# Sketched attention with a gated linear unit: larger transfers, another order of tokens, and a pipeline by units

## The chip, the cores and the metric

The kernel runs on one core of a Trainium2 chip. The metric is the device time of one execution in microseconds (us). Engines are named as in the profile: PE is TensorE (matmuls; PEld are its weight loads), DVE is VectorE, ACT is ScalarE, POOL is GpSimd, and SP issues most of the DMAs.

## What is computed

Two stages follow one another. The first is linear attention with a product sketch. For each of 4 batches and 4 heads, with 1088 tokens and a head dimension of 32:

```python
a = einsum('rd,bhsd->bhsr', S1, x); b = einsum('rd,bhsd->bhsr', S2, x)   # r = 8
phi(x) = outer(a, b) per token, 64 features
kv  = sum over tokens of phi(k) v          # 64 x 32 per head
z   = sum over tokens of phi(k)
out = (phi(q) kv) / (phi(q) z + 1e-6)
```

The heads' outputs side by side form x (4 x 1088 x 128) for the second stage:

```python
gate = sigmoid(causal depthwise convolution of x, 5 taps, conv_w)
result = (gate * (x @ w_val)) @ w_out
```

Inputs and result are float32.

## The kernel before, in words

**Tokens.** A batch has 1088 = 32 x 34 tokens, s = 34 j + T, with j in 0..31 (`J`) and T in 0..33 (`NT`). k and q are loaded with partitions (h, j) and columns (T, d). T is cut into three units (`U`) of 12, and a unit into four groups m of three chunks t: T = 12u + 3m + t. A 32x32 block transpose on VectorE (`block_transpose`, L172) turns a unit into `kT` or `qT`, with (h, d) on the partitions and, for each chunk t, 128 columns (m, j). So a chunk is 128 tokens.

**k_unit(b, u)** (L178): the block transpose; three matmuls `abk` (each in two passes, as float32) that give a and b for three chunks in a PSUM tile `ab`; a ScalarE copy of b into `b_sb`; one VectorE product `phik`, the outer products of 12 (chunk, head) pairs, 768 columns; and six `kv` matmuls (12 passes) that add phik^T v for two pairs of heads into the PSUM tile `kv`. v carries a block of ones, so that z comes out of the same matmuls.

**k_finish(b)** (L209), after a batch's three units: `rz` and the `zs` matmuls fold z with S2 into the third part of `rhsq` (by a ScalarE copy), so that a matmul with `rhsq` gives a, b and a factor c with sum of a*c = the denominator. Then `kvb` (kv masked, bf16), `wg` (kv times the convolution's taps: attention output and convolution become one matmul), and `kw` = kv w_val by a transpose and two matmuls.

**q_phi(b, u)** (L253): block transpose, three `abq` matmuls, the copy `a_sb`, then on VectorE `prod` = a*c, its row sum `den`, the reciprocal `rden`, `an` = a/den and the outer products `phiq` (bf16). Six TensorE transposes put phiq into the PSUM tile `pt`, and one ScalarE copy into `phiT`, columns ordered by T, with a halo of four T in front. For u = 2 two GpSimd copies fill that halo from the batch's last four T, moved by one j.

**q_out(b, u)** (L303), for T = 12u to 12u + 11: ten `g_ps` matmuls (five taps, two head pairs) over shifted columns of phiT, two `v_ps` matmuls with kw, the sigmoid `gate`, the VectorE product `gv`, three `o_ps` matmuls with w_out, the copy `o_sb`, and four DMAs to the output, one for each m.

**Order.** The text runs the three k units of batch 0 and k_finish(0), then for each batch q_phi 2, q_phi 0, k unit 0 of the next batch, q_out 0, q_phi 1, and so on (L347 to L363). Each engine executes its own list of instructions in order, with semaphores between engines. That list is not the order of the text: the framework plans it, by its own costs for each instruction, by the readiness of inputs and free buffers, and gives what stands earlier in the text precedence. Tiles of the pool `work` have three buffers (`o_sb` among them). In PSUM there are 2 buffers for `ab`, 1 for `kv`, 2 for `pt`, 3 for the rest (`ps_g`).

**Loads** go through SP's queue in the text's order: for each batch three for k, 24 for v (`load_v`, L84, 24 KB each) and three for q; the stores follow on the same queue. ScalarE's queue has the eight small S_blk loads (S1 and S2 transposed by the access pattern, into a block-diagonal matrix), s_l2 and wm; GpSimd's has the two weights, cast to bf16. GpSimd clears and fills the constants first (L75 to L163).

## Time and profile before

| | |
|---|---|
| median of 3 runs | 118.78 us (118.59 to 119.14) |
| the profiled execution | 118.95 us |
| its span, first to last instruction | 117.2 us |
| mean granted TensorE clock | 0.885 |
| DMA | 9.29 MB, 17544 packets, 12928 of them under 512 bytes |

A profile is one execution. A row such as "27.20 0.66 PE L257" in order of time gives the start, the time to the end of the group, the engine and the line of the kernel; "x12" counts instructions, where a float32 matmul counts twice. A row of a group gives busy time and the mean of one in nanoseconds (ns), then the idle time of the engine ahead of it and what ended most of that. The rows "PE" and "PEclk" of the profile's second part cut the span into 40 slices of 2.93 us and show tenths. "SPq" and "ACTq" are the parts of those engines that issue DMAs and wait.

### The profile page before, as it was taken

To read this page: it belongs to the slowest core of one execution; us is meant where nothing else is said; L and a number is where in the kernel's file an instruction comes from. 1 tells how busy PE (TensorE), PEld (TensorE's weight loads), DVE (VectorE), ACT (ScalarE), POOL (GpSimd) and SP (SyncE) were. 2 spreads that over 40 slices of the span, in tenths; PEclk is the share of its full clock that TensorE was granted. 3 is DMA by queue.
4 is the path that set the end of the run, shared out by engine and by line. 5 is a ranking of instruction groups with operands and counts; after the bars stand their busy time and mean duration, and the time that the engine had idled before them with its cause. 6 is when DMAs were issued, how large, how long until landed. Compare 5 with 4: busy or idle time off the path is not lost.

```text
span 117.2 us, 1742 instructions
## 1 busy us (share of the span) xinstructions
PE 78.9 (67%) x568; PEld 64.3 (55%) x568; DVE 54.4 (46%) x125; ACT 31.7 (27%) x78; POOL 12.1 (10%) x55
## 2 busy tenths in 40 slices
PE   0009029998399559985699998665799667668720
PEld 0008029986385447954687696555699326355300
DVE  0300073516944622576648555876930511884110
ACT  0000500004155321124243401434120224476330
POOL 7909700000010000000010000010000000010000
PEclk9999999999955876999557999999756999999995
DMA  2831424832238422383222730000010022222222
GB/s 75 154 46 38 86 53 118 270 90 51 49 82 279 107 51 53 89 282 97 52 51 62 244 102 11 0 0 0 0 50 17 0 71 58 67 74 52 67 67 56
DMA packets 17544, 9.29 MB, mean 79 GB/s; under 512 B 12928, under 2 KB 17536, under 8 KB 17536
## 3 DMA queue, kind: packets, MB, share of 16 engines
q1 hardware_dynamic: 13440, 8.92, 28.6%
q10 hardware_dynamic: 3808, 0.21, 2.1%
q0 software_dynamic: 288, 0.07, 0.6%
q8 instruction: 4, 0.07, 0.3%
q14 instruction: 4, 0.03, 0.1%
HBM read 7.02 MB, written 2.23 MB: 79 GB/s over the span
## 4 chain that ended last, share of the span: by engine, by line
PE 55%; DVE 15%; DMA 10%; ACT 9%; issue 4%; ACTq 1%; SPq 1%; DVEq 0%
PE kv L200 19%; PE g_ps L309 11%; PE abq L257 8%; PE abk L184 5%; DVE phiq L274 5%; PE pt L285 5%; PE v_ps L319 4%; DMA S_blk<-in_S_dram 3%; ACT phiT L290 3%; DVE phik L192 3%; DMA k_sb<-in_k_dram 2%; DMA v_sb<-in_v_dram 2%; PE zs L220 2%; ACT gate L324 2%; DVE kT L173 2%
## 5 line engine op out<-in xcount | busy, mean ns | idle before, releaser
L184 PE MATMUL abk<-S_blk,kT 128*128 128x64 f32 x72 | 13.7, 342 | 15.4 <-DMA v_sb<-in_v_dram 8.8
L200 PE MATMUL kv<-v_sb,phik 128*128 128x96 f32 x144 | 24.1, 339 | 0.0
L200 PEld LDWEIGHTS kv<-v_sb,phik 128*128 128x128 f32 x144 | 23.4, 253 | 0.7 <-issue 0.5
L184 PEld LDWEIGHTS abk<-S_blk,kT 128*128 128x128 f32 x72 | 12.9, 259 | 16.0 <-issue 14.6
L192 DVE TENSOR_TENSOR phik<-abk,b_sb 128x768 f32<-128x768 f32 x12 | 11.4, 955 | 15.7 <-ACT b_sb L188 15.7
L309 PE MATMUL g_ps<-phiT,wg 128*64 128x384 bf16 x120 | 14.8, 379 | 2.0 <-ACT phiT L290 1.5
L328 DVE TENSOR_TENSOR gv<-gate,v_ps 128x384 bf16<-128x384 bf16 x12 | 6.6, 553 | 16.3 <-PE v_ps L319 9.3
L285 PE MATMUL pt<-identity,phiq 128*128 128x128 bf16 x72 | 7.3, 250 | 9.6 <-DVE phiq L274 9.6
L290 ACT COPY phiT<-pt 128x768 bf16<-128x768 bf16 x12 | 9.6, 799 | 13.4 <-PE pt L285 13.3
L257 PE MATMUL abq<-rhsq,qT 128*128 128x96 f32 x72 | 12.0, 307 | 0.5 <-ACT rhsq L224 0.5
L285 PEld LDWEIGHTS <-phiq 128*128 128x128 bf16 x72 | 5.4, 114 | 11.3 <-DVE phiq L274 10.9
L257 PEld LDWEIGHTS abq<-rhsq,qT 128*128 128x128 f32 x72 | 10.4, 215 | 1.7 <-issue 1.1
L274 DVE TENSOR_TENSOR phiq<-an,abq 128x768 bf16<-128x768 f32 x12 | 11.2, 942 | 0.1
L298 POOL COPY phiT<-phiT 128x124 bf16<-128x124 bf16 x8 | 2.1, 290 | 88.5 <-ACT phiT L290 88.5
L324 ACT ACTIVATE gate<-g_ps 128x384 bf16<-128x384 f32 x12 | 5.9, 490 | 18.1 <-PE g_ps L309 18.1
L309 PEld LDWEIGHTS <-wg 128*64 128x64 bf16 x120 | 7.2, 122 | 5.5 <-ACT phiT L290 1.2
L319 PE MATMUL v_ps<-phiT,kw 128*128 128x384 bf16 x24 | 6.8, 370 | 1.7 <-ACT gate L324 1.7
L173 DVE STREAM_TRANSPOSE kT<-k_sb 128x384 f32<-128x384 f32 x12 | 6.7, 566 | 2.6 <-DMA k_sb<-in_k_dram 2.6
L264 DVE TENSOR_TENSOR prod<-a_sb,abq 128x96 f32<-128x96 f32 x12 | 3.0, 253 | 8.9 <-ACT a_sb L261 8.8
L173 DVE STREAM_TRANSPOSE qT<-q_sb 128x384 f32<-128x384 f32 x12 | 6.1, 555 | 2.2 <-DMA q_sb<-in_q_dram 2.2
L339 ACT COPY o_sb<-o_ps 128x384 f32<-128x384 f32 x12 | 5.7, 478 | 5.0 <-PE o_ps L334 3.9
L334 PE MATMUL o_ps<-w_out_sb,gv 128*128 128x128 bf16 x36 | 4.1, 221 | 3.3 <-DVE gv L328 3.3
(46 smaller groups left out, 49.8 us busy)
## 6 DMA issues: line engine op xcount, KB each, us to landing
v_sb<-in_v_dram SPq DMA_DIRECT2D x88, 24.0 KB, 1.8
out_dram<-o_sb SPq DMA_DIRECT2D x44, 48.0 KB, 1.6
k_sb<-in_k_dram SPq DMA_DIRECT2D x8, 192.0 KB, 3.7
q_sb<-in_q_dram SPq DMA_DIRECT2D x8, 192.0 KB, 2.5
k_sb<-in_k_dram SPq DMA_DIRECT2D x4, 160.0 KB, 3.9
q_sb<-in_q_dram SPq DMA_DIRECT2D x4, 160.0 KB, 3.3
wm<-in_moe_conv_w_dram ACTq DMA_DIRECT2D x4, 40.0 KB, 2.7
S_blk<-in_S_dram ACTq DMA_DIRECT2D x8, 1.0 KB, 2.5
```

The source lines that it names most:

```text
L173: nc.vector.transpose(out=dst[:, u * W : (u + 1) * W].rearrange("p (t m j) -> p t m j", t=NCK, m=M4), in_=src[:, u * W : (u + 1) * W].rear ...
L184: nc.tensor.matmul(ab[:, 0:2, t, :], lhsT=chunk_of(kT[b], u, t), rhs=S_blk, start=True, stop=True)
L192: nc.vector.tensor_mul(phik, a_v.unsqueeze(3).to_broadcast([P, NCK * H, r, r]), b_v.unsqueeze(2).to_broadcast([P, NCK * H, r, r]),)
L200: nc.tensor.matmul(kv_ps[b][:, g], lhsT=phik[:, x : x + 2].rearrange("p h i j -> p (h i j)"), rhs=v_sb[b][:, u, 3 * g : 3 * g + 3, t, :], ...
L257: nc.tensor.matmul(ab[:, :, t, :], lhsT=chunk_of(qT[b], u, t), rhs=rhsq[b], start=True, stop=True)
L274: nc.vector.tensor_mul(phiq, an.unsqueeze(3).to_broadcast([P, NCK * H, r, r]), ab[:, 1].rearrange("p t (h j) -> p (t h) j", h=H) .unsqueeze(2)
L285: nc.tensor.transpose(pt[:, g, :, t, :], phiq[:, x : x + 2].rearrange("p h i j -> p (h i j)"), identity,)
L290: nc.scalar.copy(out=phiT[b][:, :, HALO + u * W : HALO + (u + 1) * W], in_=pt.rearrange("p g m t j -> p g (m t j)"),)
L309: nc.tensor.matmul(g_ps[2 * D * g : 2 * D * (g + 1), :], lhsT=wg[b][:, g, kk, :], rhs=phiT[b][:, g, off : off + W], start=(kk == 0), stop= ...
L319: nc.tensor.matmul(v_ps, lhsT=kw[b][:, g, :], rhs=phiT[b][:, g, c0 : c0 + W], start=(g == 0), stop=(g == 1),)
L324: nc.scalar.activation(out=gate.rearrange("p m t j -> p (m t j)"), in_=g_ps, func=ACT.Sigmoid)
L328: nc.vector.tensor_mul(gv.rearrange("p t m j -> p m t j"), gate, v_ps.rearrange("p (m t j) -> p m t j", m=M4, t=NCK),)
```

## The change

- **Tokens.** T = 9m + 3u + t. A partition group m now holds nine T of all three units; a unit takes three from each group. So the k and q tiles keep T in order, and v's tile is laid out by (x, 9 T, d). phiT stays ordered by T, so its copy from `pt` is scattered over the groups and done in two instructions, and each q_out needs the columns of all three units of its batch.
- **Transfers.** k and q come by one DMA a batch (k of batch 0 in three units, the last with a remainder), v by eight; six output units go by one DMA each, the other six by four.
- **S.** S1 and S2 are loaded as rows (`s_nat`), transposed by TensorE, and spread over the block diagonal `S3` by two VectorE products with a head mask. S3 has a third block of zeros, so abk has 96 columns.
- **Shared outer products.** In k_unit ScalarE copies a and b (`ab_sb`); VectorE makes the products of two chunks (`phik`, 512 columns) and GpSimd those of the third (`phip`, 256 columns).
- **Denominators.** `ac` copies a and c; GpSimd makes `prod` and `an`, VectorE keeps `den` and `rden`. q_phi is split: `q_den` up to `an`, `q_phi` from `phiq` on.
- **k_finish.** ScalarE copies kv to `kvs`; GpSimd makes `kvb` and `wg` of it; `kw` is one matmul with a masked w_val of 256 columns, and one copy.
- **Order.** One loop over 19 steps with, in step s, q_den of unit s - 3, k_unit of unit s, q_phi of unit s - 4, q_out of unit s - 7, and k_finish after each third k unit.
- **Others.** The pool of `ab` has 3 buffers, `pt` 1. A sigmoid on a dummy column stands early on ScalarE. The constants' memsets on GpSimd are put in another order, and the s_l2 and wm loads come after them in the text.

```diff
-    J, NT, U, TU, M4, NCK = 32, 34, 3, 12, 4, 3
+    J, NT, U, M4, NCK = 32, 34, 3, 4, 3
+    TU = M4 * NCK
+    TM = U * NCK
...
+    def load_all(src, dst, b):
+        nc.sync.dma_start(out=dst[:, : NT * D], in_=kq_rows(src, b))
...
+    load_unit(k, k_sb[0], 0, 0)
+    for x, Sx in enumerate((S1, S2)):
+        nc.scalar.dma_start(
+            out=s_nat[x * r : (x + 1) * r], in_=Sx.unsqueeze(1).to_broadcast([r, H, D])
+        )
+    for u in range(1, U):
+        load_unit(k, k_sb[0], 0, u)
+    load_v(0)
+    load_all(q, q_sb[0], 0)
...
+    nc.scalar.activation(out=warm, in_=warm, func=ACT.Sigmoid)
+    for b in range(B):
+        nc.gpsimd.memset(k_sb[b][:, NT * D :], 0.0)
+        nc.gpsimd.memset(v_sb[b][:, 2:6:3, :, :], 1.0)
+        nc.gpsimd.memset(v_sb[b][3 * J :, :, NT - 3 * TM :, :], 0.0)
+        if b == 0:
+            nc.gpsimd.memset(s_l2, 0.0)
+            nc.gpsimd.memset(wm, 0.0)
...
+    st_ps = ps_g.tile([P, 2, r], F32, tag="g", name="st_ps")
+    nc.tensor.transpose(
+        st_ps.rearrange("p x r -> p (x r)"), s_nat.rearrange("p h d -> p (h d)"), identf
+    )
...
+        nc.vector.tensor_mul(
+            S3[:, x].rearrange("p (h r) -> p h r", h=H),
+            st_ps[:, x].unsqueeze(1).to_broadcast([P, H, r]),
+            hm.unsqueeze(2).to_broadcast([P, H, r]),
+        )
...
     for b in range(1, B):
-        for u in range(U):
-            load_qk(k[b], k_sb[b], u)
+        load_all(k, k_sb[b], b)
         load_v(b)
-        for u in range(U):
-            load_qk(q[b], q_sb[b], u)
+        load_all(q, q_sb[b], b)
...
+        ab_sb = work.tile([P, 2, NCK * HR], F32, tag="ab_sb", name="ab_sb")
+        nc.scalar.copy(out=ab_sb, in_=ab[:, 0:2].rearrange("p x t c -> p x (t c)"))
...
+        outer(nc.vector, phik, ab[:, 0, :nd].rearrange("p t (h i) -> p (t h) i", h=H), ab_sb[:, 1], 0, nd * H)
+        outer(
+            nc.gpsimd, phip, ab_sb[:, 0].rearrange("p (x i) -> p x i", i=r)[:, nd * H :], ab_sb[:, 1],
+            nd * H, H,
         )
...
-        kvb = work.tile([P, 2, 2, D], BF16, tag="kvb", name="kvb")
-        nc.vector.tensor_mul(
-            kvb, kv[:, :, 0:2, :], m64.unsqueeze(1).to_broadcast([P, 2, 2, D])
+        kvs = work.tile([P, 2, 2 * D], F32, tag="kvs", name="kvs")
+        nc.scalar.copy(out=kvs, in_=kv[:, :, 0:2, :].rearrange("p g x d -> p g (x d)"))
+        kvb = work.tile([P, 2, 2 * D], BF16, tag="kvb", name="kvb")
+        nc.gpsimd.tensor_mul(
+            kvb, kvs, m64.rearrange("p x d -> p (x d)").unsqueeze(1).to_broadcast([P, 2, 2 * D])
         )
...
+        kw_ps = ps_g.tile([P, 2, P], F32, tag="g", name="kw_ps")
+        nc.tensor.matmul(kw_ps, lhsT=kvt, rhs=w_val_sb, start=True, stop=True)
...
-        a_sb = work.tile([P, NCK * H, r], F32, tag="a_sb", name="a_sb")
-        nc.scalar.copy(out=a_sb, in_=ab[:, 0].rearrange("p t (h i) -> p (t h) i", h=H))
+        ac = work.tile([P, 2, NCK * H, r], F32, tag="ac", name="ac")
+        nc.scalar.copy(out=ac, in_=ab[:, 0:3:2].rearrange("p x t (h i) -> p x (t h) i", h=H))
...
+        nc.gpsimd.tensor_mul(prod[:, :, 0:r], ac[:, 0], ac[:, 1])
...
-        nc.vector.tensor_mul(an, a_sb, rden.unsqueeze(2).to_broadcast([P, NCK * H, r]))
+        nc.gpsimd.tensor_mul(an, ac[:, 0], rden.unsqueeze(2).to_broadcast([P, NCK * H, r]))
...
-        nc.scalar.copy(
-            out=phiT[b][:, :, HALO + u * W : HALO + (u + 1) * W],
-            in_=pt.rearrange("p g m t j -> p g (m t j)"),
-        )
+        for g in range(2):
+            nc.scalar.copy(
+                out=phiT[b][:, g, HALO:].rearrange("p (m u x) -> p m u x", m=M4, u=U)[:, :, u],
+                in_=pt[:, g].rearrange("p m t j -> p m (t j)"),
+            )
...
+        if u < U - 1 and not last:
+            nc.sync.dma_start(
+                out=o_d[:, T0 : T0 + TU, :].rearrange("j (m t) e -> m j (t e)", m=M4),
+                in_=o_sb.rearrange("p t e -> p (t e)"),
+            )
+            return
...
+    N = B * U
+    LQ, LP, LO = U, U + 1, 2 * U + 1
+    for s in range(N + LO):
+        if 0 <= s - LQ < N:
+            q_den(*divmod(s - LQ, U))
+        if s < N:
+            k_unit(*divmod(s, U))
+        if 0 <= s - LP < N:
+            q_phi(*divmod(s - LP, U))
+        if 0 <= s - LO < N:
+            q_out(*divmod(s - LO, U))
+        if s < N and s % U == U - 1:
+            k_finish(s // U)
```

## The prediction

> **What bounds the kernel now.** I read the page's totals first, then busy time by stage (cut where each batch's first abq matmul starts), then the order of time.

> ```profile
> PE 78.9 (67%) x568; PEld 64.3 (55%) x568; DVE 54.4 (46%) x125; ACT 31.7 (27%) x78; POOL 12.1 (10%) x55
> ```
> ```profile
> 18.10:27.20 9.10, 8.51 (x44) 8.10 (x43) 3.85 (x9) 0.57 (x3) 0.00 (x0) 1.00 0.56 158
> 27.20:51.10 23.90, 18.25 (x127) 14.82 (x127) 13.12 (x32) 7.63 (x19) 0.52 (x2) 0.79 0.40 105
> 51.10:72.20 21.10, 18.20 (x142) 14.82 (x143) 13.11 (x32) 6.50 (x17) 0.52 (x2) 0.84 0.39 108
> 72.20:98.20 26.00, 19.08 (x142) 15.92 (x142) 13.43 (x32) 7.14 (x19) 0.52 (x2) 0.87 0.08 21
> 98.20:110.60 12.40, 9.21 (x86) 6.10 (x87) 6.71 (x18) 6.73 (x16) 0.52 (x2) 1.00 0.24 61
> ```
> The second list has, by stretch, its length and the busy time of PE, weight loads, DVE, ACT, POOL, then the granted clock. TensorE is the engine nearest to its limit, in every batch; no other passes 62% of a batch. But 27.2 us go by before the first abq, the batches take 23.9, 21.1 and 26.0 us for like work, and the clock is below 1 in all three. Each has a cause in the order of time. The start, two steps of the chain of waits and then the rows in order of time (start, length, work):

> ```profile
> 0.81 2.51 DMA k_sb<-in_k_dram
> ...
> 3.35 3.46 DMA S_blk<-in_S_dram
> ```
> ```profile
> 1.04 5.45 ACTq L100 DMA_DIRECT2D S_blk<-in_S_dram  x8
> 6.89 3.15 ACTq L110 DMA_DIRECT2D s_l<-in_S_dram  x4
> 10.13 2.71 ACTq L116 DMA_DIRECT2D wm<-in_moe_conv_w_dram  x4
> 12.87 1.28 ACT L188 ACT_TABLE_LOAD   x1 [12.87 <-DMA v_sb<-in_v_dram]
> 14.16 0.38 ACT L188 COPY b_sb<-abk 128x96 f32<-128x96 f32 x2
> 18.19 7.74 PE L200 MATMUL kv<-v_sb,phik 128*128 128x96 f32 x36
> 27.20 0.66 PE L257 MATMUL abq<-rhsq,qT 128*128 128x96 f32 x4 [0.30 <-ACT rhsq L224]
> ```
> ScalarE issues 16 DMAs and loads a table before its first copy, at 14.16; the kv matmuls, 215 ns each, start only at 18.19. (The granted clock there reads 1.00, while the same 36 take 6.76 in a stretch at half clock, below. So I take the matmuls' own pace for the first stage.) Batch 2 has the SP queue behind it:

> ```profile
> 50.78 12.11 SPq L92 DMA_DIRECT2D v_sb<-in_v_dram  x24
> 64.43 50.86 SPq L344 DMA_DIRECT2D out_dram<-o_sb  x48
> ```
> ```profile
> out_dram<-o_sb SPq DMA_DIRECT2D x44, 48.0 KB, 1.6
> ```
> ```profile
> 64.38 0.33 PE L334 MATMUL o_ps<-w_out_sb,gv 128*128 128x128 bf16 x3
> 85.37 0.49 ACT L339 COPY o_sb<-o_ps 128x384 f32<-128x384 f32 x1
> ```
> The 120 loads, all ahead of the first store, keep SP until 64.4 (a store itself lands in 1.6). Only three o_sb exist, so the fourth copy stands at 85.37, 21 us after its o_ps, and the three ps_g banks stay filled. The planner orders the engines: abk and kv are written in turn by unit, yet the kv of batch 0 and of batch 3 run as one lump of 36.

> **Prices of TensorE.** From the chain of waits and the kv lines by stretch, first at full, then at half clock:

> ```profile
> 78.93 0.51 PE pt L285 x6
> 79.44 0.70 PE abq L257 x6
> 80.13 0.66 PE abk L184 x6
> ...
> 94.12 0.34 PE o_ps L334 x3
> ...
> 91.40 0.95 PE g_ps L309 x10
> ```
> ```profile
> 66.90:71.10 4.20, 4.12 (x34) 3.84 (x34) 1.00 0.35 90
> ```
> ```profile
> 56.70 0.82 PE pt L285 x6
> ...
> 59.44 1.33 PE abq L257 x6
> 60.77 1.74 PE g_ps L309 x10
> ...
> 66.63 0.43 PE v_ps L319 x2
> ...
> 71.31 0.63 PE zs L220 x4
> ...
> 84.64 6.76 PE kv L200 x36
> ```
> A unit at full clock: abq 0.70, abk 0.66, kv 12 x 4.12/34 = 1.45, pt 0.51, g 0.95, v 0.43, o 0.34, together 5.04. A k_finish: zs 0.63 and some 0.4 for the transpose and kw, an estimate: 1.0. At half clock the unit is 1.33 + 1.33 + 2.25 + 0.82 + 1.74 + 0.75 (v scaled like g) + 0.34 = 8.56, 1.7 times as much.

> Batch 1 (21.1 us) thus did 3 x 5.04 + 1.0 = 16.1 us of full-clock work: 76%. Its mean clock of 0.84 lost 0.16 x 21.1 = 3.4 us; without it the share is 16.1 / 17.7 = 91%. Over the whole body, 27.2 to 110.6, the work is 9 k units x 2.11 + 12 q units x 2.93 + 3 x 1.0 = 57.2 in 83.4 us: 69%.

> **The change part by part.**

> *The start.* Two s_nat DMAs replace eight; at 5.45/8 = 0.68 us each the second is issued by 2.4, and with a landing of 2.5 (the k load takes 2.51) there by 5, against 3.35 + 3.46 = 6.8. One transpose (bounded by pt's 0.1 each and a lone matmul's 0.3) and two small DVE products (near rz, under 0.3 each) make S3 by about 5.6. k's first unit now comes in 384-byte pieces, four times as many. Between 2.5 us (same bytes) and the S_blk landing (3.46, also many small pieces), I take 3.5, so kT is done by 5 and abk (1.4 at the slow pace) by 7. The table load goes ahead under the landing DMAs. But s_l2 and wm, 3.15 + 2.71 = 5.9 us of issue, still stand before the first copy in the written order, and wait for GpSimd's memsets: from about 3.6, ScalarE is free at 9.5. The copy then comes at 9.5 instead of 14.16, phik at 10.6.

> ```profile
> L157 POOL MEMSET v_sb<- 128x576 f32 x4 | 2.3, 580 | 0.0
> ...
> L163 POOL COPY rhsq<-S_blk 128x64 f32<-128x64 f32 x4 | 1.0, 238 | 2.8 <-DMA v_sb<-in_v_dram 2.8
> ...
> L160 POOL MEMSET k_sb<- 128x64 f32 x4 | 0.6, 156 | 0.2
> ...
> L298 POOL COPY phiT<-phiT 128x124 bf16<-128x124 bf16 x8 | 2.1, 290 | 88.5 <-ACT phiT L290 88.5
> ...
> L192 DVE TENSOR_TENSOR phik<-abk,b_sb 128x768 f32<-128x768 f32 x12 | 11.4, 955 | 15.7 <-ACT b_sb L188 15.7
> ...
> L264 DVE TENSOR_TENSOR prod<-a_sb,abq 128x96 f32<-128x96 f32 x12 | 3.0, 253 | 8.9 <-ACT a_sb L261 8.8
> ```
> GpSimd's setup (these memsets four times, a third weight DMA, wider masks) is longer than now, done near 13, and phip of unit 0 stands behind it. So kv: 24 from 10.6 at 215 ns to 15.8, the last 12 to 18.4, abq 1.2 later (as now, 25.94 to 27.20): **19.6**. Early end: kv at 121 ns, GpSimd not late, 10.6 + 4.4 + 1.2 = 16.2. Late end: kv in one lump behind three phips (14.5 + 7.7 + 1.2), 23.4.

> *GpSimd's products.* No two-input product stands in GpSimd's trace. Lower bound: a memset's slope, (580 - 156)/512 = 0.83 ns an element plus 0.1. Upper: a copy's (290 - 238)/60 = 0.87 twice, one read after the other, plus 0.18. A copy is the nearer row, with two inputs in place of one, so the upper: 256 elements 0.63 us, 96 0.35, 128 0.40, 320 0.74. A unit's phip, prod and an are 1.33; a batch's kvb, two wg and the halo copies 0.40 + 1.48 + 0.52; a batch 6.4 of some 17 us. It is no bound, and DVE loses phik 768 to 512 (slope (955 - 253)/672: 0.27), prod and an (0.51) a unit. What queues behind a waiting GpSimd instruction is phip, so kv's last third, and den on DVE; each has a step's work of other kinds ahead of it.

> *ScalarE.* ab_sb and ac carry 192 columns for 96, phiT goes in two copies: some 0.08 + 0.08 + 0.16 a unit, 4 us in all over 32, beside TensorE; were it on the path, 4 us.

> *The pipeline.* q_den is now a step ahead of q_phi, q_out three behind it. That takes the 2.3 us waits of pt for phiq (den, rden, an, phiq in line) off TensorE. A third ps_ab bank carries it; ps_pt falls to one, so pt waits for the two phiT copies of the unit before, a step old: nothing, or at most 0.96 x 12 us without that cover. q_out(b,0) now needs all three q_phi of its batch; the lag covers it but for the end, where three q_out stand behind the last phiT, not two: 1.7 us, inside the share taken below.

> *k_finish.* kvb now goes through a copy of kv (0.27, as kvt's 128 columns) and GpSimd, wg too: some 2 us from kv to wg instead of 1.3. Nobody asks for wg or kw before q_out, five steps on; without that lag it would be 0.7 x 4 us. The zs path to abq is unchanged. One kw matmul replaces two.

> *SP.* 43 loads for 120, at 12.11/24 = 0.50 us, are issued by 22 us; the larger ones keep the DMA engines busy longer, some ten microseconds by the same bytes (an estimate). Stores then start when o_sb is there, so the 21 us hold goes. Stores fall from 48 to 30; the last batch keeps four a unit.

> *The end.* o_sb 0.49, four issues at 0.50, a landing 1.6, and 0.5 to the last instruction (an estimate): 4.6 behind the last o_ps.

> **The sum.** Body: 9 x 2.15 (abk at abq's price, as 96 columns) + 35.2 + 3.0 = 57.5 us. The pipeline should do better than batch 1's 76% and has light first steps and a tail against 91%. I take the middle, 83%: 69.3. So 19.6 + 69.3 + 4.6 = 93.5 of span; the profiled execution took 118.95 with a span of 117.2, 1.75 around it: **95 us**, against 118.95 (median of the runs 118.78). With 91% it is 89.2, with 76% 101.6; with the bounds of the start 85.8 to 105.4.

> **Rivals.**

> *Only the start is won.* The written order is not the order that runs (kv's lumps). If the planner undoes the steps as it did the units, the body stays at 69%: 57.5 / 0.69 = 83.3, so 109 us. Against it: SP's block, which made batch 2 the longest, goes in any order.

> *GpSimd held off by DVE.* If each of the 24 transposes (0.57 us) delays a product that TensorE waits for, 13.7 us come on top, 109. [...]

> *Slower: the low clock.* The clock fell each time after TensorE had been thin, as these slices of 2.93 us show:

> ```profile
> PE   0009029998399559985699998665799667668720
> ...
> PEclk9999999999955876999557999999756999999995
> ```
> Slice 10 (counted from 0) has PE at 3 tenths, and 11 and 12 have the clock at 5; slices 18 and 19 are at 5 and 6, and 19 to 21 have 5, 5, 7; slices 25 to 27 (6, 6, 5) are followed by 7, 5, 6. If the finer pipeline leaves TensorE with many short gaps, low stretches join. With 91% and a low share f, the body is 57.5 x (1 + 0.69 f)/0.91; it makes up the whole 93.0 us that are left to it (118.95 less 19.6, 4.6 and 1.75) at f = 0.68. Three quarters low gives 122. Before had 0.23 low (a mean clock of 0.885); more constant work speaks against it. [...]

> **How the numbers follow.** Forecast 0.70, better than 84 us 0.04 (share above 91% and the early start), only the start 0.12, GpSimd held 0.06, low clock 0.06, no change 0.02. The range 84 to 109 holds the forecast, GpSimd held and half of the only-start case, 0.82. Half a per cent is about what a measurement can tell from no change; faster is 0.92, the same 0.02, slower 0.06.

> **What would show it.** First b_sb/ab_sb copy near 9.5 and abq near 19.6; a store before 60 us; no o_sb copy more than 3 us behind its o_ps; GpSimd's 256-element product at 0.3 to 0.63; batches of 17 to 20 us; clock above 0.9. Wrong if PE's share of a full batch falls below 70%, or GpSimd ends most of its idle time.

## The result, and the profile after

The changed kernel takes 91.83 us (median of 4 runs, 91.51 to 95.51), the kernel before beside it on the same chip 118.96 us (118.59 to 119.50). The ratio is 0.771, 95% interval 0.766 to 0.775. The forecast was 95 us, the range 84 to 109. The kernel before has two kinds of executions, of about 116.2 us at a granted clock of 0.905 and of 117 to 120 us at 0.857 to 0.892; all of them here are of the second kind, and against the first, as in the ratios below, the changed kernel has 0.789. The profiled execution took 91.90 us with a span of 90.2, at a mean granted clock of 0.982 instead of 0.885.

The totals of the page of the changed kernel, and TensorE with its clock in 40 slices of 2.26 us:

```profile
PE 68.8 (76%) x565; PEld 55.5 (62%) x565; DVE 42.4 (47%) x97; ACT 33.8 (37%) x90; POOL 37.4 (42%) x103
...
PE   0119699979699699999988599999698767666600
...
PEclk9999999999999999999999999999999999999975
```

The stretches of the changed kernel, cut where the first abq matmul of each batch starts, then the work behind them (length and busy time of PE, weight loads, DVE, ACT, POOL; then the clock, the DMA engines' share and GB/s):

```profile
20.30:33.20 12.90, 11.06 (x96) 10.02 (x96) 8.93 (x19) 4.70 (x15) 6.07 (x13) 1.00 0.80 220
33.20:47.80 14.60, 13.80 (x126) 11.76 (x126) 9.60 (x22) 7.24 (x21) 6.25 (x14) 1.00 0.06 16
47.80:65.00 17.20, 15.52 (x143) 12.74 (x143) 8.99 (x19) 8.45 (x25) 7.76 (x16) 1.00 0.13 33
65.00:75.40 10.40, 8.33 (x79) 5.55 (x79) 5.45 (x12) 5.90 (x16) 3.25 (x9) 1.00 0.15 38
75.40:85.60 10.20, 7.17 (x63) 3.22 (x63) 2.22 (x4) 4.30 (x10) 0.58 (x2) 1.00 0.30 83
```

TensorE's busy time fell from 78.9 to 68.8 us though it has nearly the same matmuls: what went is the half clock, which in the kernel before lay on 23.8 us between 32.2 and 90.2 (TensorE busy for 22.1 of them) and of which no stretch here shows any (it comes at 87.0, behind the last o_ps). The lag of q_out moves work to the end, so the first two batches are short; only the third, 17.2 us, holds three units of every kind. In the kernel before it took 26.0 us.

The start of the changed kernel in order of time (start, length, work):

```profile
7.42 2.68 ACTq L192 DMA_DIRECT2D wm<-in_moe_conv_w_dram  x4
...
6.33 4.16 PE L222 MATMUL abk<-S,kT 128*128 128x96 f32 x18 [2.31 <-DVE S L174]
...
10.14 0.76 ACT L226 COPY ab_sb<-abk 128x192 f32<-128x192 f32 x3 [6.86 <-POOL phiT L167]
...
20.34 0.46 PE L304 MATMUL abq<-rhsq,qT 128*128 128x96 f32 x2 [0.28 <-ACT rhsq L272]
```

ScalarE's first copy stands behind its own wm loads (7.42 + 2.68 = 10.10). "POOL phiT", named as what released it, is a memset of a tile that the copy doesn't read.

### The profile page after: what moved, and what is told of

Same layout as the page of the kernel before. It is cut to its first block, busy times and chain, and to the rows that moved or that the text cites. A ratio compares the mean times of both kernels' runs of the same rounds, so it can differ in the third digit from the quotient of the medians.

```text
span 90.2 us, 1666 instructions
## 1 busy us (share of the span) xinstructions
PE 68.8 (76%) x565; PEld 55.5 (62%) x565; DVE 42.4 (47%) x97; ACT 33.8 (37%) x90; POOL 37.4 (42%) x103
## 2 busy tenths in 40 slices
DMA packets 9137, 9.29 MB, mean 103 GB/s; under 512 B 4649, under 2 KB 8233, under 8 KB 9129
## 3 DMA queue, kind: packets, MB, share of 16 engines
q1 hardware_dynamic: 7112, 8.92, 35.2%
## 5 line engine op out<-in xcount | busy, mean ns | idle before, releaser
L248 PE MATMUL kv<-v_sb,phik 128*128 128x96 f32 x96 | 16.0, 316 | 2.6 <-DVE phik L229 1.8
L248 PEld LDWEIGHTS kv<-v_sb,phik 128*128 128x128 f32 x96 | 14.4, 226 | 3.7 <-DVE phik L229 3.5
L222 PE MATMUL abk<-S,kT 128*128 128x96 f32 x72 | 12.4, 315 | 3.1 <-DVE S L174 2.3
L341 ACT COPY phiT<-pt 128x384 bf16<-128x384 bf16 x24 | 10.7, 484 | 6.9 <-PE pt L335 6.9
L222 PEld LDWEIGHTS abk<-S,kT 128*128 128x128 f32 x72 | 11.0, 226 | 3.7 <-DVE S L174 2.4
L379 DVE TENSOR_TENSOR gv<-gate,v_ps 128x384 bf16<-128x384 bf16 x12 | 6.6, 551 | 11.6 <-ACT gate L375 10.4
L313 DVE TENSOR_REDUCE den<-prod 128x12 f32<-128x108 f32 x12 | 3.2, 264 | 16.1 <-POOL prod L311 16.1
L311 POOL TENSOR_TENSOR prod<-ac 128x96 f32<-128x96 f32 x12 | 4.7, 389 | 13.8 <-ACT ac L308 13.8
L229 DVE TENSOR_TENSOR phik<-abk,ab_sb 128x512 f32<-128x512 f32 x12 | 7.7, 656 | 4.3 <-ACT ab_sb L226 4.2
L229 POOL TENSOR_TENSOR phip<-ab_sb 128x256 f32<-128x256 f32 x12 | 7.4, 625 | 3.5 <-ACT ab_sb L226 3.4
L248 PE MATMUL kv<-v_sb,phip 128*128 128x96 f32 x48 | 8.5, 306 | 0.0
L308 ACT COPY ac<-abq 128x192 f32<-128x192 f32 x12 | 3.9, 322 | 9.9 <-PE abq L304 9.3
```

The costliest lines, as they stand in the source:

```text
L222: nc.tensor.matmul(ab[:, :, t, :], lhsT=chunk_of(kT[b], u, t), rhs=S3, start=True, stop=True)
L229: eng.tensor_mul(dst, a.unsqueeze(3).to_broadcast([P, n, r, r]), bb.rearrange("p (x j) -> p x j", j=r)[:, lo : lo + n] .unsqueeze(2) .to_b ...
L248: nc.tensor.matmul(kv_ps[b][:, g], lhsT=src.rearrange("p h i j -> p (h i j)"), rhs=v_sb[b][:, 3 * g : 3 * g + 3, NCK * u + t, :], start=(u ...
L341: nc.scalar.copy(out=phiT[b][:, g, HALO:].rearrange("p (m u x) -> p m u x", m=M4, u=U)[:, :, u], in_=pt[:, g].rearrange("p m t j -> p m (t ...
L379: nc.vector.tensor_mul(gv.rearrange("p t m j -> p m t j"), gate, v_ps.rearrange("p (m t j) -> p m t j", m=M4, t=NCK),)
```

## The experiments

The changed kernel was timed again beside three of the ten variants: 91.43 us (90.86 to 91.94), ratio 0.789 (0.780 to 0.797). The variants are compared with it by these ratios, in which 0.010 is 1.2 us, and by their medians where the executions lie close together. An edit can also change the order that the planner makes of the rest of the text, which matters in some cases below.

> The changed kernel once more, as the yardstick for the three beside it on the same chip: 91 to 92.5.

### The order of the steps, alone and taken back

In the kernel before, the loop of the changed kernel, with q_phi split and 3 and 1 buffers for `ab` and `pt`; transfers and engines as before. In the changed kernel, the loop of before as far as its dependences allow:

```diff
-        q_phi(b, 2)
-        q_phi(b, 0)
-        if b + 1 < B:
-            k_unit(b + 1, 0)
...
+    for s in range(N + LO):
+        if 0 <= s - LQ < N:
+            q_den(*divmod(s - LQ, U))
+        if s < N:
+            k_unit(*divmod(s, U))
```

> The kernel before with the new loop of 19 steps, q_den split from q_phi and 3 + 1 PSUM buffers for ab and pt; its loads, token order, start and VectorE products stay. If the order makes most of the body's gain, the body's share goes from 69% towards 80% but the o_sb hold stays: 105 to 110, with a clock above 0.93. If the transfers make it, 116 to 120.

> The changed kernel with an order like the old one (three k units and k_finish first, then by batch q_den and q_phi together, k units of the next batch and q_out between them); transfers, start and GpSimd's products stay. If the order carries the body: share of 76%, body 76 against 65, so 100 to 104. If the transfers carry it: 92 to 95.

The new order alone: 107.67 us (105.92 to 111.27), ratio 0.919 (0.902 to 0.935), so 0.081 x 116.2 = 9.4 us less. The old order in the changed kernel: 103.04 us (101.24 to 108.04), ratio 0.873 (0.868 to 0.877), 0.084 over the 0.789, so 9.8 us more. The order carries some 10 us either way. TensorE's waits in the changed kernel (in all, times, longest), first as it is:

```profile
PE pt L335 <- DVE phiq L324: 0.9, 3, 0.3
```

and with the old order, with its clock from the page:

```profile
PE pt L335 <- DVE phiq L324: 7.5, 5, 2.0
...
PE g_ps L360 <- POOL phiT L349: 2.3, 2, 1.4
```
```profile
PEclk9999975999999999999999999999999995555555
```

pt waits 7.5 us instead of 0.9 for phiq, g_ps 2.3 for GpSimd's halo copies, and the last seven slices run at half clock. So the order is worth these waits and what they do to the clock.

### Output tiles of their own

```diff
-        o_sb = work.tile([P, NCK, P], F32, tag="o_sb", name="o_sb")
+        o_sb = ctile([P, NCK, P], F32, f"o_sb{b}_{u}")
```

> The kernel before with twelve o_sb tiles in place of three, so that no copy of o_ps waits for a store; the stores still start behind the loads near 64 us. If the o_sb hold is a term of its own, batch 2 falls from 26.0 to the 21 of batch 1 and the last store wait (1.1) goes: 112 to 114. If TensorE is held elsewhere and the hold is harmless, 118 to 119.

114.88 us (113.70 to 116.59), ratio 0.980 (0.975 to 0.985): the hold of o_sb behind SP's loads is a term, of some 2 us (0.020 x 116.2 = 2.3). In the stretches of this variant, batch 2 and what follows it:

```profile
72.20:91.70 19.50, 15.44 (x143) 12.72 (x143) 13.38 (x31) 7.15 (x20) 0.52 (x2) 1.00 0.16 43
91.70:114.00 22.30, 13.00 (x98) 8.34 (x98) 7.26 (x19) 7.33 (x17) 0.52 (x2) 0.85 0.12 33
```

Batch 2 loses 6.5 of its 26.0 us, as the prediction's reading of 85.37 says. But the rest takes 22.3 us where it had 19.0 (98.2 to 117.2), 6.8 us of it at half clock (97.0 to 103.8), so half of the gain is given back.

### Small loads in the changed kernel

```diff
-                nc.sync.dma_start(
-                    out=v_sb[b][J * m : J * (m + 1), 3 * g : 3 * g + 2, :n, :],
+                for u in range(U):
...
+                    nc.sync.dma_start(
+                        out=v_sb[b][J * m : J * (m + 1), 3 * g : 3 * g + 2, NCK * u : NCK * u + n, :],
...
-        nc.sync.dma_start(out=dst[:, : NT * D], in_=kq_rows(src, b))
+        for lo in range(0, NT * D, TU * D):
+            hi = min(lo + TU * D, NT * D)
+            nc.sync.dma_start(out=dst[:, lo:hi], in_=s[:, lo:hi])
```

> The changed kernel with the loads cut up again, each transfer a third as large: v in 24 transfers a batch instead of 8, k and q of every batch in three instead of one. Order, engines and arithmetic are those of the changed kernel. Theory 1 (the large transfers carry nothing once the loads lie ahead of the stores): 91 to 93 us beside 91.4 of the changed kernel, and the waits of the body unchanged. Theory 2 (the number of issues on SP sets when the data come): the queue of SP takes about 0.6 us an issue, 80 more issues are up to 48 us of SP, so the loads of batch 2 and 3 come 20 us or more later than the 30.2 us at which SP was done, and the time is 95 us or more, with a wait for v_sb or k_sb inside the body.

101.83 us (101.08 to 104.74), ratio 0.872 (0.863 to 0.881): theory 2 by the time, some 10 us more, far above what the hold of o_sb explains. Theory 1 had been drawn from that hold alone. But the longest wait stands ahead of the body, not inside it as theory 2 has it, and not all of the 10 us is the loads themselves. The variant's rows in order of time, the stretch of its batch 0, and what pt waits for:

```profile
2.95 13.12 SPq L111 DMA_DIRECT2D v_sb<-in_v_dram  x24
...
16.11 1.38 SPq L102 DMA_DIRECT2D q_sb<-in_q_dram  x3
17.53 1.38 SPq L102 DMA_DIRECT2D k_sb<-in_k_dram  x3
...
15.18 0.71 PE L254 MATMUL kv<-v_sb,phik 128*128 128x96 f32 x2 [4.93 <-issue]
...
24.99 0.46 PE L310 MATMUL abq<-rhsq,qT 128*128 128x96 f32 x2 [0.28 <-ACT rhsq L278]
```
```profile
25.00:43.10 18.10, 14.06 (x96) 13.22 (x96) 8.49 (x19) 5.48 (x16) 6.63 (x15) 0.81 0.41 102
```
```profile
PE pt L341 <- DVE phiq L330: 7.1, 7, 2.2
```

An issue takes 13.12/24 = 0.55 us, so the 19th of the 24, which the first kv needs as it is the first of the last partition group, is issued near 13.3 and lands some 2 us later (2.0 is the median of these loads up to 26 us). TensorE waits 4.93 us and starts kv at 15.18 instead of 11.24 ("issue" means that the profile shows no releaser; that it is v is worked out from these times). Batch 0's q and batch 1's k are issued only from 16.1 on; in the changed kernel those two are issued at 6.92 and 9.05:

```profile
2.96 3.91 SPq L105 DMA_DIRECT2D v_sb<-in_v_dram  x8
6.92 0.59 SPq L99 DMA_DIRECT2D q_sb<-in_q_dram  x1
9.05 0.35 SPq L99 DMA_DIRECT2D k_sb<-in_k_dram  x1
...
29.76 0.43 SPq L99 DMA_DIRECT2D q_sb<-in_q_dram  x1
```

The first abq comes 4.65 us later, about as much as kv, and batch 0 takes 18.1 instead of 12.9 us. (This profiled execution took 104.74 us, 2.9 above the median. Two stretches of half clock of 3.4 us each lie in its batch 0, which the two executions with a mean clock of 0.99 can't have had, so some 3 of these 5 us are not in the 10.) The pieces are smaller as well as more, 12040 packets under 512 bytes instead of 4649, but from 6.0 to 25 us, the stretch with this wait, the DMA engines' share is 0.48 (0.83 in the changed kernel from 6.3 to 20.3), so it was the issuing that held.

The rest of the 10 us comes with another planned order. The text is that of the changed kernel, but the kv of batches 1 and 2 stand together here, all 36 of a batch with nothing between them, where the changed kernel has them in three parts; and pt waits 7.1 us for phiq instead of 0.9. The new order alone, with the small loads of the kernel before, has the same lumps:

```profile
57.23 4.21 PE L200 MATMUL kv<-v_sb,phik 128*128 128x96 f32 x36
```

So the planner spreads kv over the steps with the large loads of the changed kernel and not with the small ones, and the two parts of the change are not independent. How the rest of the 10 us divides between late loads and planned order is not shown.

### GpSimd's products on VectorE

```diff
-        nd = NCK - 1
+        nd = NCK
...
-        nc.gpsimd.tensor_mul(prod[:, :, 0:r], ac[:, 0], ac[:, 1])
+        nc.vector.tensor_mul(prod[:, :, 0:r], ac[:, 0], ac[:, 1])
```

and likewise an, kvb and wg.

> The changed kernel with phik in one product of 768 columns, prod, an, kvb and wg all on VectorE; GpSimd keeps memsets and halo copies. VectorE goes from 42 to about 57 us of 90. If its relief is no part of the gain: 90 to 94 (the start gains 1 to 2 us, as kv no longer waits behind GpSimd's memsets). If the sharing with GpSimd carries the body: above 99.

89.61 us (89.24 to 90.34), ratio 0.772 (0.766 to 0.779) where the changed kernel has 0.789; by the medians 1.8 us less than 91.43. VectorE is busy 61% of its span, which sets nothing. So the sharing brings no time and costs a little (two variants of the end, below, are 1.9 us apart by the same edit). The start is not the place. The first abq is at 19.38 instead of 20.34, but kv starts at 11.54, later than the 11.24 of the changed kernel, and in the second profile of the changed kernel, without any edit, the first abq is at 19.62:

```profile
16.65 1.34 PE L248 MATMUL kv<-v_sb,phik 128*128 128x96 f32 x8
...
19.62 0.46 PE L304 MATMUL abq<-rhsq,qT 128*128 128x96 f32 x2 [0.28 <-ACT rhsq L272]
```

These eight kv take 1.34 us, where the same eight, from 16.68 in the first profile, take 1.92: what differs is when the slow pace of the start ends. From the first abq to the last o_ps the changed kernel has 64.9 us in both profiles, this variant 62.7, and there the gain lies. Which product costs it is not shown, as the planned order differs too. What GpSimd's products took in the changed kernel, by groups:

```profile
L229 POOL TENSOR_TENSOR phip<-ab_sb 128x256 f32<-128x256 f32 x12 | 7.4, 625 | 3.5 <-ACT ab_sb L226 3.4
L281 POOL TENSOR_TENSOR wg<-kvs,wm 128x320 bf16<-128x320 f32 x8 | 6.7, 862 | 0.0
L311 POOL TENSOR_TENSOR prod<-ac 128x96 f32<-128x96 f32 x12 | 4.7, 389 | 13.8 <-ACT ac L308 13.8
L317 POOL TENSOR_TENSOR an<-ac,rden 128x96 f32<-128x96 f32 x12 | 4.2, 352 | 3.1 <-DVE rden L315 2.8
L276 POOL TENSOR_TENSOR kvb<-kvs,m 128x128 bf16<-128x128 f32 x4 | 1.8, 456 | 10.1 <-ACT kvs L274 10.1
```

### An earlier start

ScalarE's s_l2 and wm loads go to SP's queue, behind batch 0's q; GpSimd's memsets of batches 1 to 3 go behind the phip of the batch before.

```diff
-            nc.scalar.dma_start(
+            nc.sync.dma_start(
                 out=s_l2[
...
-            nc.scalar.dma_start(
+            nc.sync.dma_start(
                 out=wm[
...
+        if s % U == 2 and s // U + 1 < B:
+            clear(s // U + 1)
```

> The changed kernel with s_l2 and wm issued by SP behind batch 0's loads, and the memsets of batches 1 to 3 on GpSimd put behind phip of batch 0. The first ab_sb copy comes at 7.9 instead of 10.1 and phip at 8.5 instead of 12.5. If the first stage then runs at TensorE's slow pace of some 220 ns (54 instructions from 6.3), kv ends only 0.7 us earlier: 91. If ScalarE's issues and GpSimd's queue set its end: 2 to 4 us less, 88 to 90.

100.13 us (99.64 to 100.81), ratio 0.863 (0.856 to 0.871) against the 0.789 of the changed kernel beside it: both theories missed. The first abq did come 3.2 us earlier, at 17.17. Its rows in order of time, and its stretches from the fall of the clock on, 3.4 us each but for the last, which ends 0.2 before the return (as above; the clock is the third number from the end):

```profile
17.17 0.64 PE L312 MATMUL abq<-rhsq,qT 128*128 128x96 f32 x4
...
22.05 0.82 PE L343 MATMUL pt<-identity,phiq 128*128 128x128 bf16 x6 [3.88 <-DVE phiq L332]
22.67 1.54 PE L230 MATMUL abk<-S,kT 128*128 128x96 f32 x6
...
32.30 0.72 PE L343 MATMUL pt<-identity,phiq 128*128 128x128 bf16 x5 [1.62 <-DVE phiq L332]
```
```profile
19.20:22.62 3.42, 0.57 (x6) 0.57 (x7) 1.97 (x5) 0.00 (x0) 1.81 (x3) 0.50 0.98 336
22.62:26.03 3.41, 3.41 (x19) 3.41 (x17) 1.47 (x3) 1.50 (x4) 0.73 (x2) 0.50 0.83 163
26.03:29.45 3.42, 3.42 (x17) 3.26 (x17) 2.31 (x5) 0.64 (x2) 1.61 (x4) 0.50 0.69 244
29.45:32.86 3.41, 1.79 (x15) 1.55 (x13) 2.40 (x5) 1.18 (x3) 0.97 (x2) 0.50 0.97 259
32.86:36.27 3.41, 3.41 (x18) 3.41 (x17) 0.79 (x2) 0.00 (x0) 0.00 (x0) 0.50 0.44 151
36.27:39.45 3.18, 3.18 (x17) 3.18 (x16) 0.00 (x0) 0.00 (x0) 0.00 (x0) 0.50 0.00 0
```

TensorE waited 3.88 us for the first phiq, and from 19.2 to 39.6 the clock was at half: six abk matmuls took 1.54 us, where the changed kernel has 0.83 to 0.91. It fell 1 us into the wait, not at its end, and the low stretch of 20.5 us is six times 3.41, the step on which the clock of the kernel before changes as well (last section). TensorE was busy throughout the second, third and fifth of the stretches above (3.41, 3.42 and 3.41 us), and the clock came back only behind the sixth. What brings it down or back is not shown.

First I held GpSimd for the cause: its `an`, which phiq needs, stood behind two wg products of 0.86 us. The same start with every product on VectorE tests that.

> The variant of the earlier start (ScalarE's two loads on SP, the clears of the later batches behind), 100.13 us, with every product of GpSimd moved to VectorE. Theory 1 (what cost the 8.7 us there was TensorE's 3.88 us wait for the first phiq behind GpSimd's two wg products, after which the granted clock stayed near 0.6 for some 16 us): on VectorE the products don't queue behind wg on GpSimd, no wait near 22 us is over 1.5 us, the clock stays over 0.95 and the time is 86 to 89 us, below the 89.6 of the kernel with all products on VectorE and the old start. Theory 2 (the loads of s_l2 and wm that now stand behind batch 0's on SP come too late, whoever multiplies): a wait for wm of about the same length stays, and the time is 97 to 101 us.

91.51 us (90.61 to 93.00), ratio 0.778 (0.775 to 0.782): 8.6 us less by the medians, but neither theory, as it is 1 to 2 us above the same products with the late start (89.61), and the wait is still there. In order of time:

```profile
18.60 0.43 SPq L99 DMA_DIRECT2D k_sb<-in_k_dram  x1
...
20.34 0.95 DVE L327 TENSOR_TENSOR phiq<-an,abq 128x768 bf16<-128x768 f32 x1
21.21 1.49 DVE L219 STREAM_TRANSPOSE kT<-k_sb 128x384 f32<-128x384 f32 x3
21.35 0.82 PE L338 MATMUL pt<-identity,phiq 128*128 128x128 bf16 x6 [3.37 <-DVE phiq L327]
```

GpSimd's queue was 0.5 of the 3.88 us. For the rest, TensorE had nothing else to do. In the changed kernel kT of batch 1 is transposed from 13.83 on and its abk fills the time of den, rden, an and phiq:

```profile
13.83 1.50 DVE L211 STREAM_TRANSPOSE kT<-k_sb 128x384 f32<-128x384 f32 x3
```

Here the eight small loads of s_l2 and wm hold SP from 7.24 to 12.74, so batch 1's k is issued at 12.79 (9.05 in the changed kernel), and the planner put its transposes behind phiq and its abk behind pt. With GpSimd out, the clock was at half for only 6.8 us, 19.4 to 26.3 (twice 3.4). That is 13.7 us less of half clock, at half the pace up to 6.8 us, so most of the 8.6 (an estimate). Why the low stretch is three times as long with GpSimd's products, the runs don't show; the planned orders of the two variants differ too. A second wait for phiq (1.62 us near 31) lies inside it, but the two stretches ahead of that, 3.41 and 3.42 us with TensorE busy throughout, had not brought the clock back either.

### A warm TensorE

```diff
+    wz = ctile([P, 512], BF16, "wz")
+    nc.vector.memset(wz, 0.0)
...
+    busy(9)     # nine 512-column matmuls of zeros ahead of the transpose of S
```

> The changed kernel with nine matmuls of zeros (bf16, 512 columns, into a spare PSUM tile) on TensorE ahead of the transpose of S. If the slow pace of the first stage is a clock that activity raises, abk and kv of batch 0 take 120 ns instead of 220 and kv ends behind phip near 15 instead of 19.2: 87 to 89. If the pace is set by the loads that land in that stage, 91.5 to 92.5.

91.90 us (91.33 to 95.22): no gain, and yet it was work ahead of them that the slow first matmuls lacked. The variant in order of time:

```profile
1.79 3.57 PE L175 MATMUL wps<-wz 128*128 128x512 bf16 x9 [1.79 <-DVE wz L170]
...
6.16 2.25 PE L232 MATMUL abk<-S,kT 128*128 128x96 f32 x18 [0.64 <-DVE S L184]
11.18 1.67 PE L258 MATMUL kv<-v_sb,phik 128*128 128x96 f32 x8 [2.77 <-DVE phik L239]
```

The 18 abk take 2.25 us instead of 4.16, 125 ns each instead of 231. Then TensorE waits 2.77 us, as ScalarE's first copy is still at 10, and the kv run at 1.67/8 = 209 ns again. From 11.6 to 18.4 this variant's record has the clock at 0.50, and eight kv take 1.92 us there, as long as those of the changed kernel at 14.12, whose record reads 1.00. The time saved lies ahead of a wait that ends when it did.

### The end

```diff
-            q_out(*divmod(s - LO, U))
+            q_gate(*divmod(s - LO, U))
+            if s - LO < N - 4:
+                q_fin(*divmod(s - LO, U))
+            elif s - LO > N - 4:
+                q_fin(*divmod(s - LO - 1, U))
```

q_fin is o_ps, its copy and its stores; for the last four units it is written behind the next unit's g_ps.

> The changed kernel with the o_ps part of the last four units written behind the g_ps part of the next unit. In the tail each unit takes 2.45 us, 1.7 of it TensorE's work. If the written order decides there, the waits of o_ps for gv (0.74 each) go: 2 to 3 us less, 89 to 90. If the three ps_g buffers hold the next g_ps anyway: 91.5 to 92.5.

90.35 us (89.57 to 91.01) against 91.43, with ranges that just overlap (90.86 to 91.94), ratio 0.773 (0.767 to 0.779): 1.1 us by the medians, 1.9 by the ratios. The written order does decide there, but the gain is below the 2 to 3 us expected. Together with VectorE's products:

> All products on VectorE and the o_ps matmuls of the last four units one unit later, the start as it was: 88 to 89 us if the two gains (1.8 to 2 us and 1.1 us) add up, 89.6 to 90.4 if they share a term. It is what the kernel with everything is measured against: the difference of the two is the start alone.

88.46 us (87.91 to 88.88), ratio 0.759 (0.752 to 0.766): the gains add up. By its median it is the fastest of all, faster than both kernels: its longest execution lies below the shortest of the changed kernel, 90.86. The wait of o_ps for gv, in the changed kernel and here:

```profile
PE o_ps L385 <- DVE gv L379: 3.8, 6, 0.7
...
PE o_ps L386 <- DVE gv L376: 1.5, 3, 0.6
```

> All that the runs so far point to at once: the earlier start, nine idle matmuls ahead of the transpose of S, all products on VectorE, and the o_ps matmuls of the last four units one unit later. If the gains add up, it is 89.6 of the kernel on VectorE less 1.1 of the tail, less 2 to 3 of a start that reaches the first abq near 16 instead of 19.4 us: 84 to 87 us, with a granted clock over 0.95. If the clock falls at the start again, 95 us or more, and its row shows where.

89.45 us (87.12 to 90.30), by the median no better than 88.46. Its four executions are longer the lower their mean clock, from 87.12 us at 0.953 to 90.30 at 0.908; the shortest is below the 87.91 of the variant without the new start, so whether the start gains anything when less clock is lost, one execution can't tell. The profile is of one that took 88.71. The first abq comes at 14.75, 4.9 us earlier than in the kernel without the new start, and the first pt waits 3.38 us at 19.09, with the clock at half from 19.3 to 29.5. Batch 0, from the first abq to the next batch's, takes 19.2 us instead of 14.0, so in this execution the whole gain of the start goes into that wait and its clock. In order of time, and the clock in slices of 2.18 us:

```profile
14.75 0.66 PE L317 MATMUL abq<-rhsq,qT 128*128 128x96 f32 x4
...
19.09 0.67 PE L348 MATMUL pt<-identity,phiq 128*128 128x128 bf16 x6 [3.38 <-DVE phiq L337]
```
```profile
PEclk9999999995555799999999999999999999999985
```

## Why the prediction was right, and where it wasn't

**The start** was put at 19.6 and came at 20.34 (19.62 in the second profile), by the steps given: ScalarE free at 10.10 (9.5), the copy at 10.14, phip behind GpSimd's setup at 12.48 (near 13), kv at the slow pace. What the sum didn't see is what makes an earlier abq worth having. It took the start as a term that adds to the body. The early starts show that it doesn't: at 17 and at 14.8 us the loads and the plan of batch 1 are not there, and the time comes back as a wait and a low clock (3.88 us and 20.5 us at half, 3.38 and 10.2).

**The body** was put at 83% of full-clock work, 69.3 us; from 20.34 to 85.6 it took 65.3, which is 57.5/65.3 = 88%. That is the mis-sized term: the only full batch did 3 x 5.08 + 1.0 = 16.2 us of work in 17.2, 94%, above the upper bound of 91% that I had from batch 1 without its low clock. (A part of this is the price: kv took 1.34 us a unit from 56.82 to 58.16, not 1.45, and TensorE was busy 15.52 of the 17.2, 90%.) The middle was too low because I let part of the old waits and low clock remain, and pt's waits for phiq all but went (from 9.6 us to 0.9). The sign "batches of 17 to 20 us" missed: 12.9, 14.6 and 17.2, since the lag moves q_out from the first batches to a tail of 10.2 us with 7.17 busy.

**The end**: 4.6 behind the last o_ps, measured 90.2 less 85.6 = 4.6. Span 20.3 + 65.3 + 4.6 = 90.2, and 1.7 around it.

**GpSimd's products**, by the upper bound of its copies: 0.63 for 256 elements (0.625 measured), 0.35 for 96 (0.389 and 0.352), 0.40 for 128 (0.456), 0.74 for 320 (0.862, 16% more). That GpSimd is no bound was right, and so was that VectorE's relief gives nothing; the step that failed is that each product has cover: without them the body is 2.2 us shorter (62.7 instead of 64.9), though which of them costs it stays open and the planned order differs too, and in the early start `an` stood behind wg ahead of the long wait.

**SP** was put at 22 us for its last load, and it came at 30.2: the 0.50 us of an issue holds, but eight v loads of batch 3 take 6.8, 3.1 of them one wait that ended with a transfer of k (the DMA share is 0.80 until 33). No step needed them earlier. The 21 us hold of o_sb was read rightly, and its going is worth some 2 us. What I missed is the larger half of "few transfers": with small loads the first kv waits for its own v and the first abq is at 25.0, and the planner makes another order. The sum contains that gain (its start has q and v on time) but gives it to ScalarE's issue alone.

**The rivals.** "Only the start is won" fell: the body changed most. Its fear, that the planner undoes the steps, was right for kv with small loads. "GpSimd held off by DVE" fell: its products take what its copies said, and taking them away saves 2 us, not 14. "The low clock" did not come in this kernel, but in a variant: one wait of 3.88 us and the 20.5 us of half clock that came with it cost the early start more than 8 us against the changed kernel.

By parts, then: the order some 10 us, the fewer loads some 10 with the planned order that comes with them, the sharing with GpSimd 2 us lost, of 0.211 x 116.2 = 24.5 in all. These are rough shares, as the order and the loads are not independent. The remaining 5 to 7 are not taken apart: the transposed S with fewer issues on ScalarE (its first copy 14.16 to 10.14), the larger stores, and what the parts do to each other.

## What to carry to other kernels

Price a set of small DMAs by when its last piece is issued and by what stands behind it in the queue (here 24 issues of 0.55 us held the first kv back by 4 us and the next q and k by 9), not only by bytes, and look whether the planned order changed with it. An earlier stage is worth something only when the stage behind it has its data and its place in the plan; otherwise the gain turns into one wait, and here waits of 3.37, 3.38 and 3.88 us on TensorE came with 6.8, 10.2 and 20.5 us of half clock. Sharing with an idle engine brought nothing here, where the engine that is relieved didn't set the pace: with all products on it VectorE was busy 61% of its span, and the time was 1.8 us shorter.
